# A two-layer MLP's second activation moved from GpSimd to VectorE, and a planner's costs changed with it

## The chip, the cores and the metric

The kernel runs on one core of a Trainium2 chip. The metric is device time in microseconds (us) for one execution, from three runs of each kernel. Engines are named as in the profile: PE (TensorE matmul), PEld (TensorE weight load), DVE (VectorE), ACT (ScalarE), POOL (GpSimd), SP (the queue that issues the DMAs).

## The reference, cut to what matters

Clustered attention (2 batches, 8 heads, 768 tokens, head size 64) gives 1536 tokens of 512 features. Two MLP layers follow, each 512 to 2048 to 512. The change concerns the activation of the second:

```
def _moe2_ref(x, w_in, w_out, alpha):
    h = x @ w_in
    g = np.maximum(h, 0.0) + alpha * np.minimum(h, 0.0)
    return (g @ w_out).astype(np.float32)
```

alpha has one value for each of the 2048 hidden features.

## The kernel before, in words

**Numbers.** A product in float32 is made of three float16 products, since each operand is kept as a high and a low half. So each tile that feeds TensorE costs ACT a rounding to float16 and DVE a subtraction that gives the low half.

**Stages.** Attention, layer 1 and the conversion of the second layer's weights overlap in the first 540 us or so. The second layer works on three blocks of 512 tokens (j = 0, 1, 2). Block 0 is done plainly (`plain_in`, matmuls at L1428). Blocks 1 and 2 use a Winograd-Strassen scheme (`wino_in`): their weights are combined by DVE (`wino_ops`, L1313 to L1324, halves at L943), their tokens by `split_x2` (L1349 on ACT, L1350 and L1369 on DVE). Each block of the two has four groups of four features' rows. A group is seven products of 12 matmuls with 256 columns (L1452). The first product is read out of PSUM by ACT (L1471), the others by five additions (L1461) and two scaled additions (L1463) on DVE. These leave four tiles h of 128x512 in SBUF. The product tiles rotate over four PSUM banks (the names w, of which there are two, x and m), so a product cannot begin before the one four places earlier has been read.

**The activation.** `act` turns each h into g. In `wino_in` an h tile holds two feature blocks of 256 tokens each, and each block has its own column of alpha; POOL makes min(h, 0) times alpha in two instructions, one for a block (L1401). DVE then adds max(h, 0) (L1409), ACT rounds it to float16 (L1412), DVE makes the low half (L1413). For `plain_in` one DVE instruction makes the negative part (L1396), and POOL has no part in it. `layer2_out` multiplies g by the output weights: 48 matmuls of 512 columns for a group (L1495), into PSUM banks of their own (s). Four buffers hold g.

**The order of the work.** The program text is not the order on the engines. `plan_order` gives every instruction a cost, plays the program on a model of the engines, and fixes each engine's order. It plays it 60 more times (`PLAN_ROUNDS`) with priorities from the play before, run backwards, with a little random noise; the order with the earliest modelled end is kept. An engine then works through its list strictly in order. The costs that matter here are `Plan.costs`: 0.145 + n/955 us for a DVE tensor instruction of n elements a partition, 0.19 + n/1205 us for ACT, 0.19 + n/1215 + 0.08 us for this POOL instruction (for 256 elements 0.48 us).

`OUT_LAG` says how many groups `layer2_out` is written behind `wino_in` in the program text, from which the first play takes its priorities; what must wait for what is the same with either value.

Of the kernel before, what the change touches and what calls it, by code (L numbers as in the profile page):

```python
# [17 lines left out]
ALU = mybir.AluOpType  # L18
# [22 lines left out]
EXP_ON = ("aaaaaaaa", "aaaaaaaa", "aaaaaaaa", "aaaaaaaa")  # L41
P_LO_DVE = range(96)

MN_ON = "p"
OUT_LAG = 3
READERS = 6
PLAN_ROUNDS = 60
MASK = 2.0 ** 15
# [3 lines left out]
class Plan:  # L52
# [27 lines left out]
    def costs(self, i):  # L80
        aps = [a for a in list(i.ins) + list(i.outs) if hasattr(a, "bass_ap")]
        n = max(self.size(a) for a in aps) if aps else 1
        kind, e = type(i).__name__, self.engine(i)
        wide = all(a.dtype in (F16, BF16) for a in aps)
        ptr = sum(hasattr(a, "bass_ap") for a in list(i.ins)[1:]) if n > 1 else 0
        if kind == "InstTensorScalarPtr":
            ptr = sum(self.size(a) == 1 for a in i.ins if hasattr(a, "bass_ap")) if n > 1 else 0
        many = len(list(i.outs)) > 1
        if e == "PE":
            mv = [a for a in i.ins if hasattr(a, "bass_ap")][0]  # L90
            return (max(0.025, 0.001 + self.size(mv) * (8 if mv.dtype == F32 else 1) / 2330.0),)
        if e == "DVE":
            if kind == "InstTensorCopy":
                return (0.15 + n / (3840.0 if wide else 1920.0),)
            if kind == "InstMemset":
                return (0.06 + n / 1000.0,)
            return (0.145 + n / 955.0 + (0.06 * ptr if kind == "InstTensorScalarPtr" else 0) + 0.06 * many,)
        if e == "Activation":
            return (0.19 + n / 1205.0 + 0.09 * min(1, ptr) + (0.06 if many else 0),)
        if e == "Pool":  # L100
            if kind == "InstTensorTensor":
                return (0.19 + n / 530.0,)
            return ((0.1 if kind == "InstMemset" else 0.19) + n / 1215.0 + 0.08 * min(1, ptr),)
        n = max(self.size(a) for a in aps)
        if kind == "InstDmaTransposeAnt":
            return (1.3 if n < 1400 else 1.42, 1.3, n / 750.0)
        rows = [a for a in i.ins][0]
        run = list(rows.ap)[-1][1] * 4
        rate = 395.0 if run >= 4096 else 350.0 if run >= 2048 else 380.0
        return (0.47, 1.3, n * 512 / 1000.0 / rate)  # L110
# [86 lines left out]

    def improve(self, rounds):

        noise = Random(1)  # L200
        best = self.run(list(range(len(self.ins))))
        back = self.mirror()
        for _ in range(rounds):
            back.run([noise.gauss(0, 0.1) - t for t in self.ended])
            best = min(best, self.run([noise.gauss(0, 0.1) - t for t in back.ended]), key=lambda x: x[0])
        return best

    def run(self, prio):
        import heapq
# [108 lines left out]
def plan_order(tc, nc, starts):  # L318
    plan = Plan(list(nc.cur_bb.bb.instructions))
    place = {i.name: n for n, i in enumerate(plan.ins)}  # L320
    for a, b in starts:
        plan.order_only[place[a]].append(place[b])
    end, order = plan.improve(PLAN_ROUNDS)
    for line in order:
        for a, b in zip(line, line[1:]):
            tc.add_manual_dep(
                plan.ins[b], plan.ins[a].name,
                mybir.DependencyInfo(mybir.DependencyClass.NoSync, mybir.DependencyReason.DATA),
                reason="planned order",
            )  # L330
    return end
# [3 lines left out]
def cluster_attention_silu_prelu(  # L335
# [20 lines left out]
    nc = tc.nc  # L356
# [77 lines left out]
    def col(n):  # L434
        a = stat[:, nstat[0]:nstat[0] + n]
        nstat[0] += n
        assert nstat[0] <= NSTAT
        return a
# [5 lines left out]
    al_sb = col(KF)  # L444
# [68 lines left out]
    def bc(a, n):  # L513
        return a.unsqueeze(2).to_broadcast([128, a.shape[1], n])
# [821 lines left out]
    def split_x2(j):  # L1336
        x2 = view(o_x2, F32, NC2, KD, N2)
        junk = view(X_OPS[j][0], BF16, N2) if j else x2_parts(j)[0][:, 0].bitcast(BF16)
        ss = scr(KD)
        for kd in range(KD):  # L1340
            nc.scalar.activation(
                out=junk, in_=x2[:, j, kd], func=ACTF.Square, accum_out=ss[:, kd:kd + 1]
            )
        tot = all_sum([ss[:, kd:kd + 1] for kd in range(KD)], "h" if j else "s")
        s, inv = scr(1), l2[:, 2 + j:3 + j]
        pow2_scale(tot, 1, 15, None, s, inv)

        def part(src, hi, lo):
            nc.scalar.activation(out=hi, in_=src, func=ACTF.Copy, scale=s)  # L1349
            nc.vector.scalar_tensor_tensor(  # L1350
                out=lo, in0=src, scalar=s, in1=hi, op0=ALU.mult, op1=ALU.subtract
            )

        if j == 0:
            hi, lo = x2_parts(j)
            for kd in range(KD):
                part(x2[:, j, kd], hi[:, kd], lo[:, kd])
            return
        b11, b12, b21, b22 = (
            x2[:, j, 2 * kh:2 * kh + 2, N2 // 2 * th:N2 // 2 * (th + 1)]  # L1360
            for kh in range(2) for th in range(2)
        )

        def op(src, o):
            d = view(X_OPS[j][o], F16, 2, KD // 2, N2 // 2)
            part(src, d[:, 0], d[:, 1])

        def two(out, a, b, f=ALU.subtract):
            nc.vector.tensor_tensor(out=out, in0=a, in1=b, op=f)  # L1369

        op(b11, 0)
        two(b11, b12, b11)
        two(b12, b22, b12)
        op(b21, 1)
        op(b22, 2)
        two(b22, b11, b22)
        op(b22, 5)
        op(b12, 6)
        op(b11, 4)
        two(b21, b21, b22, ALU.add)  # L1380
        op(b21, 3)
# [12 lines left out]
    def act(h, out, mn, scale, f, gf):  # L1394
        if len(f) == 1:
            nc.vector.tensor_scalar(  # L1396
                mn, h, 0.0, al_sb[:, f[0]:f[0] + 1], op0=ALU.min, op1=ALU.mult
            )
        elif MN_ON == "p":
            for i, ff in enumerate(f):  # L1400
                nc.gpsimd.tensor_scalar(  # L1401
                    mn[:, i], h[:, i], 0.0, al_sb[:, ff:ff + 1], op0=ALU.min, op1=ALU.mult
                )
        else:
            nc.vector.scalar_tensor_tensor(
                out=mn, in0=h, scalar=0.0, in1=bc(al_sb[:, f[0]:f[0] + 2], N2 // 2),
                op0=ALU.min, op1=ALU.mult,
            )
        nc.vector.scalar_tensor_tensor(  # L1409
            out=gf, in0=h, scalar=0.0, in1=mn, op0=ALU.max, op1=ALU.add  # L1410
        )
        nc.scalar.activation(out=out[0], in_=gf, func=ACTF.Copy, scale=scale)  # L1412
        nc.vector.scalar_tensor_tensor(  # L1413
            out=out[1], in0=gf, scalar=scale, in1=out[0], op0=ALU.mult, op1=ALU.subtract
        )
# [69 lines left out]
    def layer2_out(n):  # L1485
        j, i = groups[n]
        first, last = i == 0, i == KF // 4 - 1
        g = g_buf(n)
        acc = [bank_s[t // 2][:, t % 2] for t in range(4)]
        for q, f in enumerate(features(n)):  # L1490
            wo = out_piece(o_w, f // 2)
            for t in range(4):
                k = 0
                for a, bb in ((0, 0), (0, 1), (1, 0)):
                    nc.tensor.matmul(  # L1495
                        out=acc[t], lhsT=g[:, q, a, t * 128:(t + 1) * 128], rhs=wo[:, bb, f % 2],
                        start=(first and q == 0 and k == 0), stop=(last and q == 3 and k == 2),
                    )
                    k += 1
        if not last:  # L1500
            return
        eo = l2[:, 6 + j:7 + j]
        nc.vector.tensor_scalar(
            eo, l2[:, 2 + j:3 + j], w2["in"].inv_smin, w2["out"].inv, op0=ALU.mult, op1=ALU.mult
        )
        nc.vector.tensor_tensor(out=eo, in0=eo, in1=l2[:, 1:2], op=ALU.mult)
        for t in range(4):
            ob = view(slots[1 + t % 2] + 2 * KB * (t // 2), F32, DM)
            nc.scalar.activation(out=ob, in_=acc[t], func=ACTF.Copy, scale=eo)
            r = j * (N2 // 128) + t  # L1510
            nc.sync.dma_start(
                out=out.rearrange("(b p t) d -> b t p d", b=B, t=T)[r // T, r % T], in_=ob
            )
# [55 lines left out]
    NG = KF // 4  # L1569
    for n in range(len(groups) + OUT_LAG):  # L1570
        if n < NG:
# [8 lines left out]
        if n == 2 * NG - 1:  # L1580
            split_x2(2)
        if n >= OUT_LAG:
            layer2_out(n - OUT_LAG)
    plan_order(tc, nc, starts)
# [32 lines left out]
```

## Time and profile before

| | |
|---|---|
| median of 3 runs | 782.05 us (781.56 to 782.7) |
| profiled execution, its own time | 784.33 us |
| profiled execution, span on the core | 782.5 us |
| busy share of the span | PE 86%, DVE 76%, PEld 64%, ACT 62%, POOL 28% |
| DVE between 560 and 600 us | 40.0 of 40 us busy |
| POOL between 620 and 660 us | 30.8 of 40 us busy |

A share over the whole span is a mean over stages with different limits, so the stages are to be read one by one. The span is what the instructions of the core take, from the first to the last; the 1.8 us more in the execution's own time lie around it.

### The profile page before, as it was taken

How to read it: one execution, taken by the hardware profiler on the slowest of the kernel's cores; microseconds unless marked ns; L12 is line 12 of the kernel's file. 1: busy time of each engine (PE TensorE's matmuls, PEld its weight loads, DVE VectorE, ACT ScalarE, POOL GpSimd, SP SyncE). 2: the span in 40 equal slices, each digit the busy share in tenths (PEclk: the TensorE clock that was granted, in tenths of full speed). 3: DMA queues.
4: the chain of work that ended last, by engine and by line, in shares of the span. 5: the costliest groups of instructions: out<-in, count | busy, mean ns of one | idle time of the engine just before them, and what ended most of it. 6: DMA issues, size and time to landing. Idle time of an engine off the chain costs nothing.

```text
span 782.5 us, 17117 instructions
## 1 busy us (share of the span) xinstructions
PE 670.0 (86%) x7035; PEld 502.1 (64%) x7035; DVE 590.8 (76%) x1052; ACT 485.4 (62%) x779; POOL 220.6 (28%) x295
## 2 busy tenths in 40 slices
PE   1354569788989999999999999999999988999997
PEld 1233358577777878877888887764444765666643
DVE  5699999987668688867966865879999877856510
ACT  6986867967768668757765887887933424221301
POOL 4651211421502642221120110200000477655410
PEclk9996659899999999999999999999999999999999
DMA  7979999798787988997897975345000001000101
GB/s 232 311 180 310 285 227 149 139 193 143 157 137 140 182 154 151 163 170 111 141 142 132 204 186 154 117 162 214 2 1 1 1 1 54 1 1 1 54 0 54
DMA packets 237358, 100.87 MB, mean 129 GB/s; under 512 B 217312, under 2 KB 227552, under 8 KB 237280
## 3 DMA queue, kind: packets, MB, share of 16 engines
q1 hardware_dynamic: 237280, 99.78, 58.9%
q8 instruction: 55, 0.90, 0.5%
q14 instruction: 23, 0.19, 0.1%
HBM read 43.03 MB, written 3.15 MB: 59 GB/s over the span
## 4 chain that ended last, share of the span: by engine, by line
PE 35%; DVE 18%; DMA 12%; ACT 8%; POOL 5%; issue 5%; ACTq 0%; SPq 0%; POOLq 0%; DVEq 0%
PE s L1495 9%; PE w L1203 7%; PE w L1234 7%; DMA arena<-arena 6%; DVE arena L943 4%; POOL arena L1401 3%; PE x L851 3%; DMA arena<-in_moe_w_in_dram 3%; DMA arena<-in_moe_w_out_dram 3%; PE s L805 2%; PE w L1452 2%; PE s L809 2%; DVE arena L833 1%; DVE arena L1413 1%; DVE s L819 1%
## 5 line engine op out<-in xcount | busy, mean ns | idle before, releaser
L1234 PE MATMUL w<-arena 128*128 128x256 f16 (+1 forms) x1248 | 151.2, 257 | 3.6 <-DVE arena L943 2.2
L1203 PE MATMUL w<-arena 128*128 128x256 f16 (+1 forms) x1200 | 142.4, 259 | 2.4 <-DVE arena L1211 1.1
L1495 PE MATMUL s<-arena 128*128 128x512 f16 x576 | 134.0, 379 | 0.0
L1203 PEld LDWEIGHTS <-arena 128*128 128x128 f16 x1344 | 113.8, 99 | 19.9 <-issue 4.3
L1234 PEld LDWEIGHTS <-arena 128*128 128x128 f16 x1344 | 110.5, 98 | 19.1 <-DVE arena L943 3.6
L851 PE MATMUL x<-arena 128*128 128x64 f16 x1728 | 105.1, 197 | 12.6 <-DMA arena<-arena 12.2
L819 DVE TENSOR_SCALAR_CACHE_REDUCE s<-s,stat 128x768 f32<-128x768 f32 x96 | 98.0, 1021 | 20.3 <-PE s L809 17.7
L833 DVE TENSOR_TENSOR arena<-arena 128x768 f16<-128x768 f32 x96 | 95.5, 994 | 23.0 <-ACT arena L831 22.5
L824 ACT ACTIVATE arena<-s,stat 128x768 f32<-128x768 f32 x96 | 86.0, 896 | 37.3 <-DVE arena L833 22.2
L1401 POOL TENSOR_SCALAR arena<-arena,stat 128x256 f32<-128x256 f32 x64 | 82.5, 1302 | 88.0 <-issue 38.9
L851 PEld LDWEIGHTS <-arena 128*128 128x128 f16 x1728 | 88.4, 101 | 25.5 <-DMA arena<-arena 16.3
L831 ACT ACTIVATE arena<-arena 128x768 f16<-128x768 f32 x96 | 80.4, 838 | 26.3 <-DMA arena<-arena 25.9
L1495 PEld LDWEIGHTS <-arena 128*128 128x128 f16 x576 | 56.3, 98 | 61.0
L805 PE MATMUL s<-arena 80*128 80x384 f16 x192 | 68.1, 355 | 20.4 <-ACT arena L824 11.0
L1412 ACT ACTIVATE arena<-arena,stat 128x512 f16<-128x512 f32 x48 | 33.9, 719 | 80.4 <-DVE arena L1409 80.3
L1452 PEld LDWEIGHTS <-arena 128*128 128x128 f16 x672 | 65.6, 98 | 27.3 <-issue 12.8
L809 PE MATMUL s<-arena 128*128 128x384 f16 x192 | 68.3, 356 | 0.0
L455 POOL TENSOR_SCALAR stat<-stat 128x1 int32<-128x1 int32 (+1 forms) x41 | 10.8, 267 | 203.2 <-DVE stat L450 138.3
L1452 PE MATMUL w<-arena 128*128 128x256 f16 x336 | 55.6, 272 | 3.2 <-ACT arena L1471 1.3
L943 DVE SCALAR_TENSOR_TENSOR arena<-arena,stat 128x1024 f16<-128x1024 f32 x40 | 52.0, 1315 | 7.9 <-ACT arena L942 7.9
L942 ACT ACTIVATE arena<-arena,stat 128x1024 f16<-128x1024 f32 x40 | 45.8, 1170 | 19.1 <-DVE arena L1322 6.9
L927 DVE SCALAR_TENSOR_TENSOR arena<-arena 128x1024 int32<-128x1024 int32 x32 | 39.2, 1224 | 23.2 <-ACT arena L920 22.9
(176 smaller groups left out, 1107.8 us busy)
## 6 DMA issues: line engine op xcount, KB each, us to landing
arena<-in_moe_w_in_dram SPq DMA_DIRECT2D x16, 1024.0 KB, 6.5
arena<-in_moe_w_out_dram SPq DMA_DIRECT2D x16, 1024.0 KB, 6.5
arena<-in_k_dram SPq DMA_DIRECT2D x8, 384.0 KB, 4.0
arena<-in_q_dram SPq DMA_DIRECT2D x6, 512.0 KB, 5.0
arena<-in_v_dram SPq DMA_DIRECT2D x8, 384.0 KB, 5.4
out_dram<-arena SPq DMA_DIRECT2D x12, 256.0 KB, 2.1
arena<-arena SPq DMA_TRANSPOSE x149, 4.1
arena<-in_centroids_dram SPq DMA_DIRECT2D x1, 32.0 KB, 3.1
```

The costliest lines, as they stand in the source:

```text
L805: nc.tensor.matmul(out=sc[:, j, :hs], lhsT=qt2[0:D + C, h], rhs=kt2[0:D + C, h % 2, j * hs:(j + 1) * hs], start=True, stop=False,)
L809: nc.tensor.matmul(out=sc[:, j, :hs], lhsT=qt1[:, h], rhs=kt1[:, h % 2, j * hs:(j + 1) * hs], start=False, stop=True,)
L819: nc.vector.tensor_scalar(sc[:, :, :hs], sc[:, :, :hs], nd_cols[:, H * (n % 2) + h:H * (n % 2) + h + 1], None, op0=ALU.mult, op1=ALU.min, ...
L824: nc.scalar.activation(out=view(o, F32, 2, hs), in_=sc[:, :, :hs], func=ACTF.Exp, scale=-1.0, bias=bias, accum_out=sums[n % 2][:, h:h + 1],)
L833: en.tensor_tensor(out=hl[:, 1], in0=p, in1=hl[:, 0], op=ALU.subtract)
L851: nc.tensor.matmul(out=x_ps[0][:, h], lhsT=pt[:, ph * T + t], rhs=vt[:, h % 2, t, vh], start=(i == 0), stop=(i == 3 * T - 1),)
L943: nc.vector.scalar_tensor_tensor(out=lo, in0=t, scalar=s, in1=hi, op0=ALU.mult, op1=ALU.subtract)
L1203: nc.tensor.matmul(out=hp[:, ff], lhsT=wi[ff][:, a, kd], rhs=mov(bb, kd), start=(i == 0), stop=(i == 3 * KD - 1),)
L1234: nc.tensor.matmul(out=acc, lhsT=wo[:, a, f % 2, dt * 128:(dt + 1) * 128], rhs=g[:, f, bb], start=(i == 0), stop=(i == 3 * KF - 1),)
L1401: nc.gpsimd.tensor_scalar(mn[:, i], h[:, i], 0.0, al_sb[:, ff:ff + 1], op0=ALU.min, op1=ALU.mult)
L1452: nc.tensor.matmul(out=hp[:, ff], lhsT=a_[:, a, kd, at + 128 * ff:at + 128 * ff + 128], rhs=b_[:, bb, kd], start=(k == 0), stop=(k == 5),)
L1495: nc.tensor.matmul(out=acc[t], lhsT=g[:, q, a, t * 128:(t + 1) * 128], rhs=wo[:, bb, f % 2], start=(first and q == 0 and k == 0), stop=(la ...
```

## The change

In the blocks of `wino_in` the negative part is made by one DVE instruction for both halves of h. alpha is given to it as a second tensor operand, each of two columns repeated along 256 tokens without being stored so. The POOL branch and its switch go. The planner's cost for ACT instructions of 1024 elements and more rises by 0.1 us (and the 0.09 us for a scalar from memory is dropped for these), its noise starts from another seed, and `OUT_LAG` goes from 3 to 2. How the best play is picked is written otherwise and does the same.

```
-MN_ON = "p"
-OUT_LAG = 3
+OUT_LAG = 2
...
         if e == "Activation":
-            return (0.19 + n / 1205.0 + 0.09 * min(1, ptr) + (0.06 if many else 0),)
+            return (0.19 + n / 1205.0 + (0.1 if n >= 1024 else 0) + 0.09 * min(1, ptr) * (n < 1024) + (0.06 if many else 0),)
...
-        noise = Random(1)
-        best = self.run(list(range(len(self.ins))))
+        noise = Random(3)
+        found = [self.run(list(range(len(self.ins))))]
         back = self.mirror()
         for _ in range(rounds):
             back.run([noise.gauss(0, 0.1) - t for t in self.ended])
-            best = min(best, self.run([noise.gauss(0, 0.1) - t for t in back.ended]), key=lambda x: x[0])
-        return best
+            found.append(self.run([noise.gauss(0, 0.1) - t for t in back.ended]))
+        return min(found, key=lambda x: x[0])
...
             nc.vector.tensor_scalar(
                 mn, h, 0.0, al_sb[:, f[0]:f[0] + 1], op0=ALU.min, op1=ALU.mult
             )
-        elif MN_ON == "p":
-            for i, ff in enumerate(f):
-                nc.gpsimd.tensor_scalar(
-                    mn[:, i], h[:, i], 0.0, al_sb[:, ff:ff + 1], op0=ALU.min, op1=ALU.mult
-                )
         else:
             nc.vector.scalar_tensor_tensor(
                 out=mn, in0=h, scalar=0.0, in1=bc(al_sb[:, f[0]:f[0] + 2], N2 // 2),
```

The plan is made anew, so the order moves on every engine from the first microseconds on. Lines of the changed kernel stand one lower in the planner's part and up to L1396, and six lower from L1403 on: the new instruction is L1399, the additions of products are L1455 and L1457, and L1409, L1412, L1413 become L1403, L1406, L1407.

On POOL, the end of the program before. L455 and L458 make the power-of-two scale of a token block, here that of block 2, and L1401 is the negative part:

```order
L455 TENSOR_SCALAR stat<-stat 128x1
L458 TENSOR_SCALAR stat<-stat 128x1
L1401 TENSOR_SCALAR arena<-arena,stat 128x256 x26
L455 TENSOR_SCALAR stat<-stat 128x1
L458 TENSOR_SCALAR stat<-stat 128x1
L1401 TENSOR_SCALAR arena<-arena,stat 128x256 x38
```

In the changed kernel the 64 instructions of L1401 are gone, and the scale of block 2 follows that of block 1 with nothing between.

On DVE, where the first group of the first Winograd block begins; before (L943 and L1320 are what is left of the weights' combinations, L1503 a scale):

```order
L1461 TENSOR_TENSOR arena<-w_69,arena 128x512
L1320 SCALAR_TENSOR_TENSOR arena<-arena,stat 128x1024
L1463 SCALAR_TENSOR_TENSOR arena<-m,stat,arena 128x512
L1461 TENSOR_TENSOR arena<-x,arena 128x512
L1461 TENSOR_TENSOR arena<-w_68,arena 128x512
L1409 SCALAR_TENSOR_TENSOR arena<-arena 128x512
L1461 TENSOR_TENSOR arena<-w_68,arena 128x512
L1461 TENSOR_TENSOR arena<-w_69,arena 128x512
L1463 SCALAR_TENSOR_TENSOR arena<-m,stat,arena 128x512
```

and now:

```order
L1455 TENSOR_TENSOR arena<-w_69,arena 128x512
L942 SCALAR_TENSOR_TENSOR arena<-arena,stat 128x1024
L1457 SCALAR_TENSOR_TENSOR arena<-m,stat,arena 128x512
L1455 TENSOR_TENSOR arena<-x,arena 128x512
L1455 TENSOR_TENSOR arena<-w_68,arena 128x512
L1399 SCALAR_TENSOR_TENSOR arena<-arena,stat 128x512
L1455 TENSOR_TENSOR arena<-w_68,arena 128x512
L1455 TENSOR_TENSOR arena<-w_69,arena 128x512
L1403 SCALAR_TENSOR_TENSOR arena<-arena 128x512
L1399 SCALAR_TENSOR_TENSOR arena<-arena,stat 128x512 x2
L1457 SCALAR_TENSOR_TENSOR arena<-m,stat,arena 128x512
```

The seven reads of PSUM keep their order; one L1399 now stands ahead of the fifth of them and two more ahead of the seventh, and the addition of the positive part (L1409, now L1403) comes two reads later.

On ACT, at the end of attention, where the conversion of the second layer's weights begins (L916, L920, L957 and their successors L915, L919, L956 are its 1024-element instructions, L824 and L831, now L823 and L830, the exponential and the rounding of attention); before:

```order
L916 ACTIVATE arena<-arena 128x1024
L1210 ACTIVATE arena<-m,stat 128x512
L920 ACTIVATE arena<-arena 128x1024
L831 ACTIVATE arena<-arena 128x768
L1210 ACTIVATE arena<-w_69,stat 128x512
L1214 ACTIVATE arena<-arena 128x2x256
L916 ACTIVATE arena<-arena 128x1024
L920 ACTIVATE arena<-arena 128x1024
L831 ACTIVATE arena<-arena 128x768
L824 ACTIVATE arena,stat<-s_64,stat 128x768
```

and now:

```order
L915 ACTIVATE arena<-arena 128x1024
L919 ACTIVATE arena<-arena 128x1024
L1209 ACTIVATE arena<-m,stat 128x512
L915 ACTIVATE arena<-arena 128x1024
L919 ACTIVATE arena<-arena 128x1024
L830 ACTIVATE arena<-arena 128x768
L823 ACTIVATE arena,stat<-s_64,stat 128x768
L956 ACTIVATE arena,stat<-arena 128x1024
```

Attention's last exponential now has two pairs of the weights' conversion close ahead of it, with one layer-1 instruction (L1209) between them, where before an attention rounding and three layer-1 instructions stood among the pairs.

## Rows read from the trace of the kernel before

**Rows 1.** Busy time by stage (us), with instruction counts and PE clock.

```profile
core 0: us, PE busy (x) PEld busy (x) DVE busy (x) ACT busy (x) POOL busy (x), PEclk, DMA share, GB/s
440.00:540.00 100.00, 92.26 (x870) 74.10 (x870) 73.66 (x97) 82.35 (x119) 8.71 (x22) 1.00 0.55 163
600.00:680.00 80.00, 68.94 (x517) 49.95 (x515) 65.83 (x99) 30.81 (x47) 46.55 (x36) 1.00 0.04 14
680.00:760.00 80.00, 80.00 (x497) 48.49 (x496) 39.56 (x57) 15.08 (x22) 36.26 (x30) 1.00 0.04 14
```

**Rows 2.** Waits of PE, 600 to 680: total us, times, longest.

```profile
PE m L1452 <- DVE arena L1461: 3.7, 3, 2.4
PE w L508 <- DVE arena L1461: 3.3, 1, 3.3
PE w L1452 <- ACT arena L1471: 1.3, 1, 1.3
```

**Rows 3.** Timeline, 641 to 654: start, us, engine, instruction, [idle before, releaser].

```profile
641.70 0.69 DVE L1409 SCALAR_TENSOR_TENSOR arena<-arena 128x512 f32<-128x512 f32 x1 [2.68 <-POOL arena L1401]
...
643.05 0.38 PE L1452 MATMUL m<-arena 128*128 128x256 f16 x2 [2.42 <-DVE arena L1461]
...
651.93 0.69 DVE L1409 SCALAR_TENSOR_TENSOR arena<-arena 128x512 f32<-128x512 f32 x1 [2.08 <-POOL arena L1401]
...
653.27 0.16 PE L508 MATMUL w<-stat,arena 128*128 128x1 bf16 x1 [3.29 <-DVE arena L1461]
```

**Rows 4.** Waits of DVE, 600 to 760, the longest.

```profile
DVE arena L1409 <- POOL arena L1401: 29.4, 23, 2.7
```

**Rows 5.** Lines L1401 and L737 of POOL: ns minimum/median/maximum, first and last start.

```profile
L1401 POOL TENSOR_SCALAR arena<-arena,stat x64: 1132/1141/2218, 614.7 to 745.5; 128x256 f32<-128x256 f32 x64
...
L737 POOL TENSOR_SCALAR arena<-arena,stat x11: 691/692/692, 52.1 to 390.5; 128x512 f32<-128x512 f32 x11
```

**Rows 6.** Groups by line and shape on POOL and DVE: busy us, mean ns.

```profile
L1401 POOL TENSOR_SCALAR arena<-arena,stat 128x256 f32<-128x256 f32 x64 | 82.5, 1302 | 88.0 <-issue 38.9 <-DVE arena L1463 18.2 <-DVE arena L1461 16.2
...
L1409 DVE SCALAR_TENSOR_TENSOR arena<-arena 128x512 f32<-128x512 f32 x32 | 23.6, 744 | 29.4 <-POOL arena L1401 29.4
...
L877 DVE TENSOR_TENSOR arena<-x,stat 128x512 f32<-128x512 f32 x12 | 8.3, 688 | 4.0 <-PE x L851 3.6
...
L587 DVE TENSOR_TENSOR arena<-arena,stat 128x192 f16<-128x192 f16 x8 | 5.0, 629 | 0.1
```

**Rows 7.** Timeline of DVE, 629 to 633: successive starts, runs of two.

```profile
629.48 1.28 DVE L1409 SCALAR_TENSOR_TENSOR arena<-arena 128x512 f32<-128x512 f32 x2
630.68 0.74 DVE L1463 SCALAR_TENSOR_TENSOR arena<-w,stat,arena 128x512 f32<-128x512 f32 x1
631.34 1.40 DVE L1413 SCALAR_TENSOR_TENSOR arena<-arena,stat 128x512 f16<-128x512 f32 x2
```

**Rows 8.** Timeline of PE: runs of both kinds of matmul; first read, last run.

```profile
611.99 0.69 DVE L1461 TENSOR_TENSOR arena<-w,arena 128x512 f32<-128x512 f32 x1
...
618.90 1.47 PE L1452 MATMUL w<-arena 128*128 128x256 f16 x12
...
737.24 40.52 PE L1495 MATMUL s<-arena 128*128 128x512 f16 x187
```

**Rows 9.** Waits of ACT, 600 to 680, on POOL.

```profile
ACT arena L1349 <- POOL stat L455: 7.4, 1, 7.4
```

**Rows 10.** Groups of ACT with 1024 elements: busy us, mean ns.

```profile
L942 ACT ACTIVATE arena<-arena,stat 128x1024 f16<-128x1024 f32 x40 | 45.8, 1170 | 19.1 <-DVE arena L1322 6.9 <-POOL stat L455 5.9 <-DVE arena L1320 5.5
...
L920 ACT ACTIVATE arena<-arena 128x1024 f32<-128x1024 f32 x32 | 36.5, 1140 | 0.0
```

**Rows 11.** Waits of PE, 440 to 540, the longest.

```profile
PE s L508 <- ACT arena L957: 5.1, 5, 1.6
```

**Rows 12.** Busy time by stretch, 100 to 140; columns as in rows 1.

```profile
100.00:120.00 20.00, 13.30 (x165) 10.71 (x164) 18.59 (x35) 12.24 (x20) 2.07 (x3) 0.60 1.08 219
120.00:140.00 20.00, 18.11 (x336) 16.11 (x336) 18.77 (x49) 15.82 (x35) 4.07 (x9) 1.00 0.85 147
```

## The prediction, made before the changed kernel ran

> **What bounds the kernel now.** I read the busy time by stage first. From 440 to 540 us PE is busy 92.3 of 100 us, from 680 to 760 it never stops, and between 600 and 680 it is busy 68.9 of 80 [rows 1]. PE is the bound of the second half, all its work there has to be done whatever the order, and the 11.1 us that it loses between 600 and 680 are the largest hole. DVE has 65.8 busy us in that stretch and POOL 46.6, so none of the three is full: a hole in which no engine is full is a chain of waits. The list of PE's waits gives its end: the longest single waits are for the DVE additions that read products out of PSUM (L1461) [rows 2]. The timeline gives what is behind them. At 641.70 DVE starts an L1409 for which it had waited 2.68 us on POOL; the read that PE needs stands right behind it in DVE's list, and PE starts at 643.05 after 2.42 us idle. At 651.93 the same happens with 2.08 us, and PE starts at 653.27 after 3.29 us [rows 3]. So POOL is late, DVE waits in order, the product bank is not read, PE has no bank. Over the stage DVE waits 29.4 us for L1401, in 23 pieces [rows 4].
>
> Why POOL is late is in its duration. One L1401 takes 1.13 us at least and 1.30 in the mean [rows 5, 6], and a tile needs two; the planner's formula gives 0.48. The order before was made for a POOL more than twice as fast as the one that runs.
>
> **The change part by part.** *Removed:* 64 POOL instructions, 82.5 us [rows 6]. For one tile the chain between the last addition and L1409 loses 2 x 1.14 = 2.3 us at the median and gets back one DVE instruction.
>
> A rule speaks against the move. The measured 1.14 us for 256 elements stands beside 0.69 us for 512 elements in another POOL instruction with one tensor input [rows 5], so the time of such an instruction here hangs on its two operations and not on its elements alone. The Trainium skill (GPSIMD Engine Reference, section 4.1, Engine selection) says that one-input work on GpSimd runs at roughly line rate; at the 1.2 GHz of its section 1 that is an estimate of 0.2 us and an overhead for 256 elements. By that rule POOL would not have been late and the change would only load DVE; by the rows two instructions cost 2.3 us. The measurement decides.
>
> *Added:* 32 DVE instructions of 512 elements, both tensors in SBUF. The trace before has none with this repeated operand at this size in SBUF. The nearest is L1409, same operation form and size, 0.744 us in the mean; a repeated operand of the same helper from SBUF beside a PSUM tile (L877) takes 0.688; the worst with such an operand is L587 with 0.629 for 192 elements [rows 6], which scaled to 512 would be 1.68. I take L1409's, since L877 shows that repeating alone costs nothing. What it takes from DVE is the distance of starts: two L1409 and what follows them start 1.20 us apart, so 0.60 each, and L1463 and L1413 0.66 [rows 7]. 32 x 0.60 = 19.2 us more for DVE, all after the first product is read at 611.99 [rows 8].
>
> Does DVE then starve PE? A group of `wino_in` was 5 x 0.60 + 2 x 0.66 + 4 x (0.60 + 0.66) = 9.4 us of DVE and is now 11.8. PE's side is 187 output matmuls in 40.5 us [rows 8], 0.217 each, and half of that for 256 columns: 84 x 0.109 + 48 x 0.217 = 19.6 us. So DVE has room in every group but for the start, where PE has no output work in stock and lives on products. Their seven reads are 4.3 us of DVE for 9.2 us of PE, and the new order keeps them ahead of most of the activation. The cover is that activations may come later than reads; without it, the added 17 instructions that replace the 34 POOL ones of this stretch put 10.2 us into 14.2 idle us of DVE [rows 1], and up to all of that could come back as waits. Between 0 and 10.2 us I take 3, nearer to nothing: the two long waits that are traced to POOL alone are 5.7 of the 11.1 [rows 3], some of the small ones may have had another cause, and DVE's list is denser now. Gain of the hole: 11.1 - 3 = 8.
>
> *Also freed:* block 2's scale on POOL stood behind 26 of L1401 in the list; ACT waited 7.4 us for it once [rows 9]. This is in the hole already.
>
> *ACT's costs.* These instructions took 1.14 to 1.17 us [rows 10], the formulas gave 1.04 to 1.13 and now about 1.14 to 1.2. No instruction gets shorter; the order fits the chip better. PE's waits between 440 and 540 sum to 7.7 us [rows 1], of which 5.1 are small matmuls that wait for L957 of the weights' conversion [rows 11]. In the new order the conversion's pairs stand more densely at attention's end. That can save some of the 5.1, or hold back attention's last exponential by one pair, 2 x 1.14 = 2.3 us. I take 0, with bounds of 5 saved and 3 lost.
>
> *The new seed and OUT_LAG* add and remove nothing, and do not alter what must wait for what. They shuffle the order of the first 440 us, which no row prices; I take 0. For the bounds see the rivals.
>
> Sum: the profiled execution took 784.3 us, 2.3 above the median; 784.3 - 8 = 776.3, and against the median 782.05 - 8 = **774.0 us**.
>
> **The rivals.** *DVE gives half of it back.* If the 10.2 us added in the stretch show up as PE waits for about half of them, the gain is 2 to 5 and the time 777.5 to 780. For it: DVE is already full from 560 to 600 (the table of the profile), and the first activations stand between reads. Against: 4.3 us of reads per 9.2 us of products.
>
> *The new order also helps earlier.* Up to 5 us of the L957 waits and some of the shuffle: 765 to 771. For it: the planner's ACT and negative-part costs now agree with the rows. Against: only 7.7 us are there to be had between 440 and 540.
>
> *Slower: PE's clock rises one stretch later.* From 100 to 120 us the granted clock is 0.60 (a part of the stretch at 1.2 GHz, the rest at 2.4), and it is full from 120 to 140, once the dense layer-1 matmuls run; there PE packs 18.1 us of work into 20 [rows 12]. If the shuffled order spreads these matmuls so that this stretch is granted 1.2 GHz throughout, its 18.1 us of work need about 36, less the overlap with work that is waiting anyway: 8 to 16 us lost, which takes the whole gain: 782 to 790. It decides from about half of that stretch on. For it: the order there is new, and its first layer-1 matmuls come a little later in PE's list. Against: the same number of matmuls stands ahead of them within a few per cent.
>
> *The repeated operand is slow.* At L587's rate 32 x (1.68 - 0.60) = 34.6 us more of DVE; a group would be 16 of PE's 19.6 us and the start starved: about 785. L877 speaks against it.
>
> **How the numbers follow.** 0.2% (1.6 us) is about what a measurement of this kernel can tell from no change. Main case 771 to 777.5: 0.45. Half given back: 0.18. Earlier help: 0.19. Late clock or a like loss ahead of 540 us: 0.15, half of it within 0.2% and half slower. Slow operand: 0.03. Faster 0.82, same 0.07, slower 0.11. The range of 766 to 783 leaves out the best of the third case and most of the last two, under 2 in 10.
>
> **What would show it.** The new DVE instruction (L1399) near 0.70 us; no POOL work in the last 170 us; L1403's waits for POOL gone and its place taken by DVE's own work; PE busy over 76 of the 80 us that follow 600; the last run of output matmuls ending about 8 us earlier. Wrong, if L1399 is over 1 us, if PE's waits for L1455 stay above 6 us, or if DVE's first read of a product (before, 611.99 [rows 8]) comes more than 3 us from where it was, since then the shuffle ahead of it decided.

## The result, and the profile after

The changed kernel takes 763.46 us (median of 4 runs, 761.44 to 764.98) against 781.8 for the kernel before beside it: a ratio of 0.9765, 95% interval 0.9733 to 0.9797. It is 18.3 us faster. The forecast was 8 us faster with a range down to 766, so the direction was right, and the size was less than half of what came.

The profiled execution took 764.79 us with a span of 762.7, which is 19.8 below the span of before. Busy time of the changed kernel in the stretches of [rows 1]:

```profile
core 0: us, PE busy (x) PEld busy (x) DVE busy (x) ACT busy (x) POOL busy (x), PEclk, DMA share, GB/s
440.00:540.00 100.00, 95.14 (x851) 74.36 (x848) 75.84 (x100) 81.97 (x117) 6.26 (x22) 1.00 0.52 164
600.00:680.00 80.00, 79.58 (x581) 56.25 (x579) 75.54 (x118) 30.93 (x48) 0.34 (x2) 1.00 0.04 14
```

The hole is gone: PE is busy 79.6 of the 80 us after 600, where it was 68.9, with DVE at 75.5. The list of PE's waits between 590 and 690, which answers to [rows 2], has one line left:

```profile
PE w L1446 <- ACT arena L1465: 0.4, 1, 0.4
```

These are the addition of the positive part, which [rows 6] show as L1409 with 29.4 us of waiting for POOL, and the new DVE instruction L1399 (line, shape, busy us, mean ns | idle before):

```profile
L1403 DVE SCALAR_TENSOR_TENSOR arena<-arena 128x512 f32<-128x512 f32 x32 | 21.2, 681 | 0.1
L1399 DVE SCALAR_TENSOR_TENSOR arena<-arena,stat 128x512 f32<-128x512 f32 x32 | 21.2, 683 | 0.2
```

The repeated operand costs nothing that shows: 683 ns with it, 681 without.

Two landmarks divide the gain. PE's work is the same in both kernels, and in each of the eighteen profiled runs about 377 of its 613.5 us of work (376.5 to 377.5) stand ahead of the first landmark; work is counted as the columns of the matmuls, at least 64 for each, at 2400 a microsecond. The landmarks are the first weight load of block 0 of the second layer (before L1428, now L1422) and the last one of the output matmuls (L1495, now L1489). Lines of before come first, then those of the changed kernel; the two times ahead of the semicolon are the first and the last start:

```profile
L1428 PEld LDWEIGHTS <-arena x192: 95/98/98, 521.2 to 573.9; 128*128 128x128 f16 x192
L1495 PEld LDWEIGHTS <-arena x576: 95/98/98, 559.0 to 777.2; 128*128 128x128 f16 x192
```

```profile
L1422 PEld LDWEIGHTS <-arena x192: 95/98/98, 514.2 to 569.8; 128*128 128x128 f16 x192
L1489 PEld LDWEIGHTS <-arena x576: 95/98/98, 552.3 to 757.3; 128*128 128x128 f16 x192
```

From one landmark to the other it was 256.0 us and is 243.1, so 12.9 came there, where 8 were forecast. The first landmark stands 7.0 us earlier, where 0 was forecast. (The profiled execution of before was 2.5 us above its median, so some of the 7.0 is that execution.)

### The profile page after: what moved, and what is told of

Its sections match the earlier page's. It is cut to its first block, busy times and chain, and to the rows that moved or that the text cites. A ratio compares the mean times of both kernels' runs of the same rounds, so it can differ in the third digit from the quotient of the medians.

```text
span 762.7 us, 17062 instructions
## 1 busy us (share of the span) xinstructions
PE 668.0 (88%) x7035; PEld 502.7 (66%) x7035; DVE 600.8 (79%) x1084; ACT 483.8 (63%) x779; POOL 137.8 (18%) x231
## 4 chain that ended last, share of the span: by engine, by line
PE 41%; DVE 13%; DMA 9%; ACT 6%; issue 4%; POOL 1%; ACTq 0%; SPq 0%; POOLq 0%; DVEq 0%
PE s L1489 11%; PE w L1233 8%; PE w L1202 6%; PE w L1446 5%; DMA arena<-arena 4%; PE x L850 3%; DVE arena L942 3%; DMA arena<-in_moe_w_in_dram 3%; PE x L1446 2%; DMA arena<-in_moe_w_out_dram 2%; PE m L1446 2%; PE s L804 2%; PE s L808 2%; ACT arena L956 1%; DVE arena L1312 1%
## 5 line engine op out<-in xcount | busy, mean ns | idle before, releaser
L1489 PE MATMUL s<-arena 128*128 128x512 f16 x576 | 134.3, 379 | 0.0
L823 ACT ACTIVATE arena<-s,stat 128x768 f32<-128x768 f32 x96 | 86.0, 896 | 39.0 <-DVE s L818 19.9
L1489 PEld LDWEIGHTS <-arena 128*128 128x128 f16 x576 | 56.3, 98 | 60.5
L830 ACT ACTIVATE arena<-arena 128x768 f16<-128x768 f32 x96 | 80.3, 839 | 21.7 <-DMA arena<-arena 21.3
L1406 ACT ACTIVATE arena<-arena,stat 128x512 f16<-128x512 f32 x48 | 33.7, 717 | 75.2 <-DVE arena L1403 75.1
L454 POOL TENSOR_SCALAR stat<-stat 128x1 int32<-128x1 int32 (+1 forms) x41 | 14.4, 355 | 324.8 <-DVE stat L449 220.5
L1446 PE MATMUL w<-arena 128*128 128x256 f16 x336 | 53.6, 273 | 0.4 <-ACT arena L1465 0.4
L915 ACT ACTIVATE arena<-arena 128x1024 int32<-128x1024 uint32 x32 | 36.8, 1151 | 22.2 <-DMA arena<-in_moe_w_out_dram 11.2
## 6 DMA issues: line engine op xcount, KB each, us to landing
out_dram<-arena SPq DMA_DIRECT2D x12, 256.0 KB, 2.1
```

Of the source, the lines that this page charges most:

```text
L823: nc.scalar.activation(out=view(o, F32, 2, hs), in_=sc[:, :, :hs], func=ACTF.Exp, scale=-1.0, bias=bias, accum_out=sums[n % 2][:, h:h + 1],)
L830: nc.scalar.activation(out=hl[:, 0], in_=p, func=ACTF.Copy)
L1446: nc.tensor.matmul(out=hp[:, ff], lhsT=a_[:, a, kd, at + 128 * ff:at + 128 * ff + 128], rhs=b_[:, bb, kd], start=(k == 0), stop=(k == 5),)
L1489: nc.tensor.matmul(out=acc[t], lhsT=g[:, q, a, t * 128:(t + 1) * 128], rhs=wo[:, bb, f % 2], start=(first and q == 0 and k == 0), stop=(la ...
```

## The experiments

Theory 1 at the start was the prediction's: POOL's long instructions make the hole, and taking them away closes it. Theory 2: the planner's order makes it, and what helped was a plan made anew. From after_pool_true on, and in all runs below it but before_seed3, theory 1 is a third one: the hole comes from an order made with a wrong cost. A draw is the order that the planner makes with one seed. In the table, "told" is what the planner was told of the negative part, and "PE waits" is the sum of the list of PE's waits between 590 and 690 us. Ratios are to the kernel before on the same chip.

| run | negative part, told | seed, ACT costs | median us | ratio (95%) | landmarks, us | between | PE waits |
|---|---|---|---|---|---|---|---|
| before (profiled) | POOL, 0.48 | 1, old | 782.05 | | 521.2, 777.2 | 256.0 | 11.1 |
| changed | DVE, 0.68 | 3, new | 763.46 | 0.9765 (0.9733 to 0.9797) | 514.2, 757.3 | 243.1 | 0.4 |
| move_old_order | DVE, order of before | as before | 780.01 | 0.9972 (0.9943 to 1.0001) | 517.7, 771.8 | 254.1 | 6.7 |
| pool_new_order | POOL, order of the change | as changed | 770.13 | 0.9858 (0.9807 to 0.991) | 513.4, 762.7 | 249.3 | 4.7 |
| pool_cost_true | POOL, 1.22 | 1, old | 769.91 | 0.9858 (0.9796 to 0.992) | 521.3, 764.9 | 243.6 | 0.6 |
| after_pool_true | POOL, 1.22 | 3, new | 763.74 | 0.9783 (0.9752 to 0.9813) | 515.6, 756.9 | 241.3 | 1.2 |
| after_dve_short | DVE, 0.22 | 3, new | 768.77 | 0.9838 (0.9803 to 0.9872) | 515.6, 762.3 | 246.7 | 2.7 |
| before_act_cost | POOL, 0.48 | 1, new | 771.47 | 0.9872 (0.9839 to 0.9905) | 515.4, 764.1 | 248.7 | 6.3 |
| before_seed2 | POOL, 0.48 | 2, old | 775.94 | 0.9935 (0.99 to 0.9971) | 520.2, 770.8 | 250.6 | 6.0 |
| before_seed3 | POOL, 0.48 | 3, old | 774.99 | 0.9923 (0.9899 to 0.9947) | 513.2, 768.0 | 254.8 | 8.6 |
| before_seed4 | POOL, 0.48 | 4, old | 769.64 | 0.9842 (0.9811 to 0.9873) | 513.3, 761.9 | 248.6 | 5.2 |
| after_seed1 | DVE, 0.68 | 1, new | 766.39 | 0.9807 (0.9771 to 0.9844) | 518.2, 757.9 | 239.7 | 0.3 |
| after_seed2 | DVE, 0.68 | 2, new | 763.08 | 0.9758 (0.9696 to 0.9819) | 514.2, 757.9 | 243.7 | 0.7 |
| after_seed4 | DVE, 0.68 | 4, new | 765.09 | 0.9784 (0.9755 to 0.9812) | 513.3, 758.5 | 245.2 | 0.4 |
| after_old_act_s1 | DVE, 0.68 | 1, old | 772.35 | 0.9844 (0.9804 to 0.9883) | 522.2, 764.7 | 242.5 | 1.1 |
| after_old_act_s2 | DVE, 0.68 | 2, old | 768.56 | 0.9795 (0.9713 to 0.9878) | 514.6, 758.8 | 244.2 | 0.6 |
| after_old_act_s3 | DVE, 0.68 | 3, old | 763.1 | 0.9726 (0.9688 to 0.9763) | 512.1, 756.3 | 244.2 | 0.7 |
| after_old_act_s4 | DVE, 0.68 | 4, old | 764.77 | 0.9747 (0.9707 to 0.9787) | 514.3, 758.0 | 243.7 | 0.4 |

**The move without a new plan, and the new plan without the move.** Two kernels have their engines' orders written out as lists in place of the planner. The first keeps every list of before and puts the DVE instruction where POOL's result was awaited:

```diff
-MN_ON = "p"
+MN_ON = "d"
...
-    plan = Plan(list(nc.cur_bb.bb.instructions))
+    (the order of before as lists; each new DVE instruction right ahead of its L1409)
```

> The order of the kernel before is kept on every engine, written out as lists; only the 64 POOL instructions go, and each pair is replaced by the one DVE instruction, put into DVE's list right ahead of its L1409. OUT_LAG stays 3. Theory 1 (POOL's lateness makes the hole, the new order ahead of 515 us is worth about 7 us by itself): PE's times up to 600 us stay within 1 us of before, the hole of 11 to 13 us shrinks to 1 to 4, the time is 770 to 773. Theory 2 (the gain comes from making the plan anew, and the move alone only loads DVE in an order not made for it): at most 4 us gained, 778 to 782.

The second keeps the lists of the changed kernel and has POOL make the negative part again:

```diff
-            nc.vector.scalar_tensor_tensor(
-                out=mn, in0=h, scalar=0.0, in1=bc(al_sb[:, f[0]:f[0] + 2], N2 // 2),
-                op0=ALU.min, op1=ALU.mult,
-            )
+            for i, ff in enumerate(f):
+                nc.gpsimd.tensor_scalar(
+                    mn[:, i], h[:, i], 0.0, al_sb[:, ff:ff + 1], op0=ALU.min, op1=ALU.mult
+                )
```

> The reverse: the order of the changed kernel is kept on every engine as lists, but the negative part is made by POOL again, 64 instructions in the order of the DVE instructions that they replace, with the scale of the last token block behind 26 of them as before. Theory 1: the first 515 us keep the 7 us gain, the stretch from the first product on loses 10 us or more, since POOL takes at least 64 x 1.14 us and each tile waits 2.3 us in place of 0.7: 773 to 778. Theory 2: the loss is under 4 us: 763 to 767.

The move alone gained 2 us, at the edge of what its interval tells from nothing. In the old order DVE became what was late: busy 77.9 of the 80 us, PE 73.2. Here is the first group of that run (start, us, engine, instruction; L1490 is the new instruction, L1494 the addition of the positive part, L1546 and L1548 the reads of products):

```profile
612.21 0.67 DVE L1546 TENSOR_TENSOR arena<-w,arena 128x512 f32<-128x512 f32 x1
612.80 0.67 DVE L1490 SCALAR_TENSOR_TENSOR arena<-arena,stat 128x512 f32<-128x512 f32 x1
613.51 0.69 DVE L1494 SCALAR_TENSOR_TENSOR arena<-arena 128x512 f32<-128x512 f32 x1
614.12 1.28 DVE L1546 TENSOR_TENSOR arena<-w,arena 128x512 f32<-128x512 f32 x2
...
614.86 0.60 PE L1537 MATMUL w<-arena 128*128 128x256 f16 x4 [0.33 <-DVE arena L1546]
```

```profile
600.00:680.00 80.00, 73.17 (x528) 51.79 (x527) 77.87 (x121) 31.26 (x47) 0.34 (x2) 0.98 0.04 14
```

The pair stands between the reads, with 1.9 us from the read at 612.21 to the next at 614.12 where two reads in a row are 0.6 apart, and PE waits 0.33 us for the bank; over the list such waits come to 6.7 us.

The granted clock of 0.98 is a second loss, which the list of waits does not hold: 0.02 of 80 us is 1.6 us. PE had been busy 5.4 of the 8 us from 640 to 648, with gaps for DVE's reads. From 648.3 to 651.7 us the clock stood at the lower of its two levels, 1.2 GHz, and an output matmul took 0.63 us where it takes 0.38 at 2.4 GHz:

```profile
649.28 0.63 PE L1580 MATMUL s<-arena 128*128 128x512 f16 x1
...
651.93 0.38 PE L1580 MATMUL s<-arena 128*128 128x512 f16 x1
```

Two of the runs with other draws below have such spells too (granted 0.96 in these 80 us in before_seed3, 0.98 in before_act_cost). The other five runs with 2.7 us of waits or more have none between the landmarks, and neither has any of the ten with 1.2 us or less.

The new order with POOL in it gained 12 us. Theory 1 asked for 770 to 773 and 773 to 778 and got 780.01 and 770.13; theory 2 asked for 778 to 782 and 763 to 767. Neither fits both; the order carries more than the move.

**The cost that the planner is told.** One more line in the kernel before gives the POOL instruction about the time that it takes (1.14 us in the median and 1.30 in the mean before [rows 5, 6]):

```diff
+            if kind == "InstTensorScalarPtr" and n == 256:
+                return (1.22,)
             return ((0.1 if kind == "InstMemset" else 0.19) + n / 1215.0 + 0.08 * min(1, ptr),)
```

> The kernel before, whose planner is told 1.22 us for the POOL instruction of 256 elements in place of 0.48, and nothing else; the plan is made anew with the old seed. Theory 1 (POOL is a long chain even when it is known): a hole of 5 to 11 us stays behind the first product, and the rest shifts by a few us either way with the shuffle: 774 to 785. Theory 2 (the plan was only misinformed): PE's waits after the first product fall under 3 us, 768 to 774.

The POOL instructions stayed, at 1.43 us in the mean, and the hole closed: 243.6 us between the landmarks, 0.6 us of waits, and PE busy 79.3 of 80 us.

```profile
600.00:680.00 80.00, 79.30 (x570) 55.19 (x569) 65.05 (x98) 29.82 (x45) 45.86 (x35) 1.00 0.04 14
```

The same line in the changed kernel with POOL put back:

> The changed kernel in all but one thing: the negative part of the Winograd blocks stays on POOL, and the planner is told 1.22 us for it. Theory 1 (the hole was a wrong cost: the order was made for a POOL of 0.48 us): the hole is closed here too, PE waits under 3 us behind the first product, and the time is 762 to 769, the changed kernel's but for the shuffle. Theory 2 (POOL in itself is too slow for the chain): 5 us or more of PE waits behind the first product stay, 769 to 776.

It takes 763.74 us, the changed kernel's time. Its busy time after 600 us:

```profile
600.00:680.00 80.00, 78.82 (x575) 55.77 (x574) 61.88 (x92) 28.76 (x46) 51.05 (x40) 1.00 0.04 14
```

POOL works more in this stretch than before the change (51.1 against 46.6 us in [rows 1]), its instructions are no shorter, and PE is busy 78.8 of 80:

```profile
L1402 POOL TENSOR_SCALAR arena<-arena,stat 128x256 f32<-128x256 f32 x64 | 85.7, 1351 | 69.3 <-ACT arena L1505 28.6 <-DVE arena L1405 21.1 <-DVE arena L1459 17.0
```

What differs is where DVE's list has the addition that waits for POOL (here L1405). Before, the first L1409 stood ahead of the fifth read of the first group. In this order it stands behind all seven (L1457, L1459):

```
L1457 TENSOR_TENSOR arena<-w_68,arena 128x512
L1457 TENSOR_TENSOR arena<-w_69,arena 128x512
L1459 SCALAR_TENSOR_TENSOR arena<-m,stat,arena 128x512
L1405 SCALAR_TENSOR_TENSOR arena<-arena 128x512 x2
```

DVE still waits for POOL, 14.7 us in all where it was 29.4, but at places where PE does not need a read next.

The wrong cost was then put on the other engine. The changed kernel's planner is told 0.22 us for the new instruction:

```diff
+            if kind == "InstTensorScalarPtr" and n == 512 and any(x[0] == 0 for a in aps for x in list(a.ap)[1:]):
+                return (0.22,)
```

> The changed kernel with the wrong cost put back on the other engine: the planner is told 0.22 us for the new DVE instruction, which took 0.68. Nothing else is changed, the instructions are the same. Theory 1 (a wrong cost makes the hole): 4 us or more of PE waits come back behind the first product, 767 to 775. Theory 2 (POOL made it): under 2 us of PE waits there, 760 to 766.

It is 5.3 us slower than the changed kernel and 2.4 slower than the slowest of the four draws with the right cost, and 2.7 us of waits are back, all but 0.2 for DVE reads. The expectation of 4 us of waits was too high, and its 767 to 775 held. So an error of half a microsecond in a plan's cost made such waits on DVE too, in the one draw tried; POOL is not needed for them.

**The planner's noise and the ACT costs.** Each of these changes a seed, or one line:

```diff
-        noise = Random(1)
+        noise = Random(3)
```

> The kernel before with the planner's noise from seed 3, nothing else. Theory 1: the hole behind the first product stays (9 us or more of PE waits), and the part ahead of it moves by up to 7 us either way: 775 to 788. Theory 2 (a fresh shuffle is the gain): 763 to 772.

> The kernel before with the planner's noise from seed 2, nothing else: a second draw with the wrong POOL cost and the old ACT costs. Theory 1 (wrong POOL cost makes the hole): behind the first product 0 to 5 us are gained against before, never 10. If the ACT costs are what moved the part ahead of 515 us, that part stays within 3 us of before; if any new draw moves it, 5 to 9 us are as likely as none. 770 to 785.

> The same with seed 4: a third draw with the old costs, same expectations, 770 to 785.

```diff
-            return (0.19 + n / 1205.0 + 0.09 * min(1, ptr) + (0.06 if many else 0),)
+            return (0.19 + n / 1205.0 + (0.1 if n >= 1024 else 0) + 0.09 * min(1, ptr) * (n < 1024) + (0.06 if many else 0),)
```

> The kernel before with only the planner's ACT costs of the change (0.1 us more for 1024 elements and more); old seed, POOL, OUT_LAG 3. If these costs are what moved the part ahead of the first product, PE passes 515 us of before 4 us or more earlier; if the shuffle did it, it moves by any amount within 7 us either way. The hole behind the first product should stay (9 us or more) by theory 1: 774 to 788.

With the wrong POOL cost, all five orders (before and these four) have 5.2 to 11.1 us of PE waits after 590 and 248.6 to 256.0 us between the landmarks. So a lucky draw gets some of the hole back, none closes it. Three of the four missed what was expected, all by being faster: seed 4, 769.64 where 770 was the least, the ACT costs, 771.47 where 774 was, and seed 3 by a hair, 774.99 where 775 was. The waits missed too: 8.6 us with seed 3 and 6.3 with the ACT costs, where 9 were the least; and seed 4 gained 7.4 us between the landmarks where 5 were the most.

The changed kernel with other seeds:

> The changed kernel with the old seed of the planner's noise. Theory 1: the hole behind the first product stays closed (under 3 us of PE waits), and the part ahead of it falls anywhere within 7 us of before: 762 to 773. If the seed is what closed the hole: 772 to 782.

> The changed kernel with seed 2. Theory 1: 11 to 13 us gained behind the first product as with seeds 1 and 3. If the ACT costs moved the part ahead of 515 us, it gains 5 to 9 us here too; if it was the draw, it can be anywhere from 0 to 9: 760 to 772.

> The changed kernel with seed 4, same expectations: 11 to 13 us behind the first product, 5 to 9 us ahead of it if the ACT costs are the cause: 760 to 772.

The hole stays closed in all: 0.3 to 0.7 us of waits, 763.08 to 766.39 us. And with the old ACT costs:

> The changed kernel with the old ACT costs, seed 1. If the ACT costs are worth 3 us ahead of the first product, the four draws of this kind take 593 to 597 us in the mean until PE has done 450 of its 613.5 us of work, against 590.8 with the new costs; if they are worth nothing, 589 to 592. Behind it all four should take 166 to 168 us, as the negative part's cost is right.

> The changed kernel with the old ACT costs, seed 2: the same expectations as for seed 1, 593 to 597 us in the mean of the four draws if the costs matter, 589 to 592 if not.

> The changed kernel with the old ACT costs, seed 3, which is the change without its ACT costs: the same expectations as for seed 1; if the costs are the whole of the 7 us, this one is at 596 to 598 by itself.

> The changed kernel with the old ACT costs, seed 4: the same expectations as for seed 1, 593 to 597 us in the mean of the four draws if the costs matter, 589 to 592 if not.

Behind the first product all four are as expected. Ahead of it, the time at which PE has done 450 of its 613.5 us of work (its matmuls in their order, counted as for the landmarks, against their starts in the trace) is 597.0, 591.7, 589.2 and 590.8, 592.2 in the mean; with the new ACT costs and the same seeds 591.4, 590.6, 590.6 and 591.7, 591.1 in the mean. By seed the old costs are 5.6 and 1.1 us later, then 1.4 and 0.9 earlier. 592.2 lies between the two expectations and by itself decides for neither. But the kernel before took 784.42 us beside the four with the old costs and 781.08 to 781.82 beside the others. That is more than 0.3%, or about 2 us at this point of the run. Against the kernel before beside them the two fours come out alike, with a mean ratio of 0.978 each. The change without its ACT costs (seed 3) takes 763.1 us, the change 763.46: for this change, the ACT costs gave nothing that can be seen.

## Why the prediction was right in direction and wrong in cause and size

**What held.** PE was the bound, the hole after 600 us was the place, and it closed. The new instruction took 0.683 us where L1409's 0.744 was taken, and no time is lost to the repeated operand, so that rival fell. DVE had room for it: 75.5 of 80 us.

**The step that failed first: "So POOL is late, DVE waits in order", and "Why POOL is late is in its duration".** The waits were read rightly from [rows 3]. The cause was not the duration but that the order was made for 0.48 us, which the prediction noted and did not follow up. Given as long a duration and a cost near it, POOL costs PE 0.6 or 1.2 us of waits in the two orders tried, and with the other lines of the change the whole time is the changed kernel's, 763.74 us. The direction was right by luck in part: the move in the order of before gained 2 us, at the edge of nothing. The edit that reads as a move between engines worked because the planner's DVE formula is right for the new instruction. The prediction weighed a rule of the Trainium skill (GPSIMD Engine Reference, section 4.1, Engine selection), one-input work on GpSimd at roughly line rate. This case's traces do not agree for this instruction, which took 1.35 us in the mean for 256 elements in the last POOL run too. So POOL was as slow as the prediction had it, and yet it was not what bound the stage.

**The term that was mis-sized: "Between 0 and 10.2 us I take 3. Gain of the hole: 11.1 - 3 = 8".** It came to 12.9 us between the landmarks, with 0.4 us of waits left. The 3 would have been too little for the move by itself: in the old order the waits stayed at 6.7 of 11.1, which is the rival "DVE gives half of it back". (That rival's own numbers do not agree: half of 10.2 us given back leaves a gain of 6.0, not 2 to 5.) In an order that knows the cost, DVE at 75.5 of 80 us gives next to nothing back: the reads stand where PE needs them.

**The term at 0: "The new seed and OUT_LAG"**, with "I take 0" for the shuffle and for the ACT costs. The first landmark came 7.0 us earlier. One of the prediction's own signs of being wrong came true with it: DVE's first read of a product moved by more than 3 us, from 611.99 [rows 8] to 605.7 (the first start in this line):

```profile
L1455 DVE TENSOR_TENSOR arena<-w,arena x20: 675/681/692, 605.7 to 723.8; 128x512 f32<-128x512 f32 x20
```

The sign was to mean that the shuffle decided; it did so for about a third of the gain. Seed 3 alone in the kernel before moves the first landmark from 521.2 to 513.2. An execution of the very order of before (the first experiment) has it at 517.7, so up to 3.5 of the 7 or 8 us lie between two executions of one order. The rest goes with the draw: with the old ACT costs the landmark lies anywhere from 512.1 to 522.2 over the seeds and kernels tried. The rival "the new order also helps earlier" had this, with up to 5 us, but not together with a full closing of the hole; its 765 was the lowest time considered.

**The slower rivals.** PE's clock came no later: the dense layer-1 matmuls of the changed kernel run in the same stretch of 120 to 140 us, granted 0.98 against 1.00 [rows 12].

What stays open: whether the ACT costs are worth a microsecond or two over many draws, and what share OUT_LAG has by itself, which was not tried. Together with the move, and with the old ACT costs, it left the first landmark within 1.1 us of the kernel before's for seeds 1, 3 and 4, and 5.6 earlier for seed 2.

## What to carry to other kernels

Where an order is planned from costs, compare each cost with the trace before an instruction is moved: one line that corrected POOL's 0.48 us to 1.22 closed the same hole as the move. A wait behind an instruction says which instruction was late for the order, not that its engine is too slow; give the same work an order made with its true duration and see whether the wait stays. And a plan made anew is a change of its own: here another seed alone moved the work ahead of the edited stage by 8 us, so an edit is judged either in a frozen order or over several draws.

## What the runs showed of the hardware that was not expected

One POOL form took 1.13 us at least for 256 elements, the minimum with a zero and then a product with a value from memory, while two products, the first with a value from memory, took 0.69 for 512 [rows 5]. And the DVE instruction whose second tensor is two columns each repeated 256 times took 683 ns, as much as one with two full tensors in SBUF in the same run (681). And in three of the eight runs with 2.7 us of PE waits or more in the second layer the granted clock over the 80 us after 600 was 0.98 or 0.96, and never under 1.00 in the ten with 1.2 us or less. The kernel before, with the most waits, had 1.00, so the waits alone do not decide it; what does was not tried.
